# Summing z of the second attention layer over token tiles in fp32 on GpSimd and VectorE, in place of 64 one-column matmuls, with the instruction lists of all engines remade

## The chip, the cores and the metric

The kernel runs on one core of a Trainium2 chip. The metric is the device time of one execution in microseconds (us). All runs told here were in the fast state with a granted TensorE clock of 0.99 to 1.0. Of each kernel there is also one profiled execution, and the profiles and traces shown are of those. A verdict of "faster" or "slower" needs more than 2%; nothing here comes near that, so the questions are about single microseconds out of 431.

## The reference, cut to what matters

Two linear-attention blocks alternate with two feed-forward blocks, over 2048 tokens of width 512 (16 tiles of 128 tokens).

```python
phi = lambda t: jnp.where(t > 0, t + 1, jnp.exp(t)) + 1e-6
pq, pk = phi(q), phi(k)
kv = jnp.einsum("bhsd,bhse->bhde", pk, v)
z = jnp.einsum("bhsd->bhd", pk)                 # what the change is about
den = jnp.einsum("bhqd,bhd->bhq", pq, z)[..., None] + 1e-6
o = num / den
...
x = x + _A_ref(_layernorm(x, axis=-1), A_wqkv, A_wo)          # layer 0
x = x + _B_ref(_layernorm(x, axis=-1), B_w_gate, B_w_up, B_w_down)
x = x + _A_ref(_layernorm(x, axis=-1), A_wqkv, A_wo)          # layer 2
x = x + _B_ref(_layernorm(x, axis=-1), B_w_gate, B_w_up, B_w_down)
```

z is the sum of pk over all tokens: 512 numbers, one for each head and dimension.

## The kernel before

Every engine works through its own list of instructions, in order, and these lists are written out by hand in the source: one for TensorE and one each for ScalarE, VectorE, GpSimd and the DMA queue. In the names, the first figure is the layer; `2k5` is the K projection of tile 5, `2q13` a query projection, `2g5` four matmuls of pk against xn (the matrix G), `2z5` the four one-column matmuls of tile 5, `2d01` the denominators, `2m0` a part of the product M that stands behind z, `2s` the new final sum. A PSUM bank is one of the eight buffers that matmuls write.

```python
def z_acc(L, t):                    # before: 4 one-column matmuls for a tile
    if L not in zb:
        zb[L] = [bank(pin=True), 0]         # a PSUM bank held from first to last
    ...
    for c in range(NC):
        mm(pb, pk[t][:, c * P:(c + 1) * P], ones[:], n == 0 and c == 0, n == T - 1, ...)
    if n == T - 1:
        z_fin(L, pb)                        # VectorE: Zm = z masked by heads

def z_add(L, t):                    # there already, used only by the change
    eng = "dve" if f"{L}b{t}" in ON_ACT else "pool"
    if n == 1: op(eng, lambda v: v.tensor_copy(out=zs, in_=pk[t][:]), ...)
    else:      op(eng, lambda v: v.tensor_tensor(out=zs, in0=zs, in1=pk[t][:], op=ALU.add), ...)

def z_sum(L):                       # there already, used only by the change
    op("dve", lambda v: v.tensor_copy(out=hi, in_=zs), ...)                              # bf16 value
    op("dve", lambda v: v.tensor_tensor(out=lo, in0=zs, in1=hi, op=ALU.subtract), ...)   # remainder
    for i, src in enumerate((hi, lo)):
        for c in range(NC):
            mm(pb, src[:, c * P:(c + 1) * P], ones[:], i == 0 and c == 0, i == 1, ...)
    z_fin(L, pb)
```

## Time and profile before

| | before |
|---|---|
| time, first three runs | 431.31 us median (430.57 to 431.77) |
| span of the profiled run | 429.9 us |
| TensorE busy | 421.3 us, 98% |
| TensorE waits on record, all | under 6 us, in ten places |
| one-column matmuls of layer 2 | 64, worth 1.63 us of TensorE |

The spans of kernels differ by tenths, so I read them by stretches: the distance in the timeline of TensorE from the start of one named group to the start of another. A wait shows as a longer stretch; what comes before it does not matter.

The prediction shows the busy shares, the chain, the waits and the z stretch of this kernel. VectorE at the end of the first feed-forward layer's opening (columns: start, busy time, instruction, and in brackets the idle time before it with what ended it):

```profile
94.55 0.41 DVE L523 TENSOR_SCALAR xnB<-X,mv,rstd 128x512 bf16<-128x512 bf16 x1
95.92 0.43 DVE L733 TENSOR_TENSOR pq<-pq,RT 128x512 bf16<-128x512 bf16 x1 [0.96 <-DMA RT<-rrep]
...
96.97 0.69 DVE L788 TENSOR_TENSOR hT<-tht,pb 128x512 bf16<-128x512 f32 x1
```

VectorE stands 0.96 us in front of a multiplication whose operand a transposing DMA has yet to bring; hT, behind it in the list, comes late, and TensorE waits 0.81 us for it at 97.72. ScalarE behind z:

```profile
257.26 0.63 ACT L720 ACTIVATE rrep<-rtok 128x512 bf16<-128x512 bf16 x1 [0.27 <-DMA RT<-rrep]
258.52 0.63 ACT L720 ACTIVATE rrep<-rtok 128x512 bf16<-128x512 bf16 x1 [0.63 <-DMA RT<-rrep]
261.13 0.63 ACT L720 ACTIVATE rrep<-rtok 128x512 bf16<-128x512 bf16 x1 [1.99 <-DMA RT<-rrep]
261.67 1.06 ACT L658 ACTIVATE GT<-pb 128x512 bf16<-128x512 f32 x2
```

Three copies wait, 2.9 us in sum, because the DMA has not yet read the buffer that they write; the evacuations of G (line 658) stand behind them.

### The profile page before, as it was taken

What the parts mean: (1) busy time and instruction counts of PE and PEld (TensorE: products, weight loads), DVE (VectorE), ACT (ScalarE), POOL (GpSimd) and SP (SyncE); (2) the same over time, 40 slices, a digit from 0 to 9 for tenths busy, and PEclk for the clock granted to TensorE, in tenths of its full rate; (3) what the DMA queues carried; (4) which work ended last, traced back from release to release, by engine and by line L of the source; (5) the groups of instructions that cost most, each with busy time, mean ns of one, the idle gap of its engine ahead of it and who ended that gap; (6) DMA issues with size and microseconds to landing.
All of it is one profiled execution on the core that took longest, in us unless ns stands there. A gap on an engine that the chain in (4) does not pass through costs nothing.

```text
span 429.9 us, 6424 instructions
## 1 busy us (share of the span) xinstructions
PE 421.3 (98%) x2275; PEld 196.7 (46%) x2275; DVE 280.2 (65%) x625; ACT 205.1 (48%) x404; POOL 69.8 (16%) x192
## 2 busy tenths in 40 slices
PE   8999999999999999999999999999999999999997
PEld 6444444444444444444444454344444444444443
DVE  6856899884585476874545549977846606934752
ACT  5999885551375334344375747455322303411320
POOL 4534036210130130000212000431002000100000
PEclk9999999999999999999999999999999999999999
DMA  8748534522021021000011113222110010031001
GB/s 281 135 75 300 155 61 120 127 51 50 0 38 24 2 51 35 2 0 2 13 39 24 24 26 69 57 37 50 23 27 12 19 43 25 2 73 38 0 2 49
DMA packets 53279, 23.22 MB, mean 54 GB/s; under 512 B 46528, under 2 KB 52160, under 8 KB 53248
## 3 DMA queue, kind: packets, MB, share of 16 engines
q1 hardware_dynamic: 51408, 16.27, 17.9%
q0 software_dynamic: 1296, 6.03, 4.2%
q10 hardware_dynamic: 544, 0.52, 0.4%
q8 instruction: 18, 0.29, 0.3%
q14 instruction: 13, 0.11, 0.1%
HBM read 9.70 MB, written 2.10 MB: 27 GB/s over the span
## 4 chain that ended last, share of the span: by engine, by line
PE 84%; DMA 7%; DVE 4%; ACT 2%; issue 1%; POOL 1%; SPq 0%; ACTq 0%; DVEq 0%
PE pb L410 84%; DMA RT<-rrep 3%; DMA xnT<-xnB 2%; DMA xnT<-xnA 1%; DMA X<-in_A_x_dram 1%; ACT rrep L720 1%; DVE X L763 1%; DVE rtok L713 0%; DVE pq L574 0%; POOL rstd L512 0%; DVE tht L785 0%; DVE pq L751 0%; DVE xnB L523 0%; SPq L724 0%; ACT xnB L499 0%
## 5 line engine op out<-in xcount | busy, mean ns | idle before, releaser
L783 ACT ACTIVATE tht<-pb 128x512 f32<-128x512 f32 x112 | 65.0, 595 | 123.1 <-PE pb L410 90.1
L785 DVE SCALAR_TENSOR_TENSOR tht<-tht,pb 128x512 f32<-128x512 f32 x112 | 75.3, 684 | 64.7 <-ACT tht L783 60.4
L410 PE MATMUL pb<-xnT,Wg 128*128 128x512 bf16 x448 | 114.9, 379 | 1.0 <-DMA xnT<-xnB 1.0
L410 PE MATMUL pb<-xnT,Wu 128*128 128x512 bf16 x448 | 115.0, 379 | 0.0
L410 PE MATMUL pb<-Wd,hT 128*128 128x512 bf16 (+2 forms) x462 | 100.0, 373 | 0.8 <-DVE hT L788 0.8
L788 DVE TENSOR_TENSOR hT<-tht,pb 128x512 bf16<-128x512 f32 x112 | 73.8, 683 | 2.4
L410 PEld LDWEIGHTS pb<-Wd,hT 128*128 128x128 bf16 x462 | 44.5, 98 | 53.5 <-DVE hT L788 1.8
L410 PEld LDWEIGHTS pb<-xnT,Wg 128*128 128x128 bf16 x448 | 43.5, 98 | 53.9 <-DVE X L763 1.1
L410 PEld LDWEIGHTS pb<-xnT,Wu 128*128 128x128 bf16 x448 | 43.8, 98 | 52.9 <-issue 0.3
L512 POOL TENSOR_TENSOR rstd<-vpe,negh 128x1 f32<-128x1 f32 x64 | 37.2, 584 | 50.8 <-DVE vpe L508 49.2
L565 ACT ACTIVATE etmp<-pb 128x512 bf16<-128x512 f32 x64 | 37.1, 594 | 15.8 <-PE pb L410 8.8
L502 POOL TENSOR_SCALAR mv<-sums 128x1 f32<-128x1 f32 x55 | 12.9, 239 | 178.4 <-DVE X L763 91.5
L499 ACT ACTIVATE xnB<-X,sums 128x512 bf16<-128x512 bf16 x32 | 23.0, 718 | 20.4 <-DVE X L763 10.9
L410 PE MATMUL pb<-xnT,Wqkv 128*128 128x512 bf16 x128 | 32.0, 379 | 0.0
L410 PE MATMUL pb<-Wqkv,xnT 128*128 128x512 bf16 x128 | 31.2, 379 | 0.6 <-DMA xnT<-xnA 0.3
L410 PE MATMUL pb<-pk,xnA 128*128 128x512 bf16 x128 | 31.5, 378 | 0.0
L570 DVE TENSOR_SCALAR etmp<-etmp 128x512 bf16<-128x512 bf16 x64 | 18.0, 291 | 19.7 <-ACT etmp L565 19.3
L499 ACT ACTIVATE xnA<-X,sums 128x512 bf16<-128x512 bf16 x23 | 16.5, 717 | 29.2 <-DVE X L811 29.2
L410 PE MATMUL pb<-GT,pq 128*128 128x512 bf16 x128 | 30.2, 379 | 0.0
L763 DVE SCALAR_TENSOR_TENSOR X<-pb,X 128x512 bf16<-128x512 f32 x32 | 21.4, 684 | 8.2 <-PE pb L410 8.2
L811 DVE SCALAR_TENSOR_TENSOR X<-pb,X 128x512 bf16<-128x512 f32 x16 | 11.0, 689 | 19.4 <-PE pb L410 19.4
L568 ACT ACTIVATE pq<-pb,onep 128x512 bf16<-128x512 f32 x25 | 17.1, 688 | 7.3 <-PE pb L410 7.2
(70 smaller groups left out, 292.3 us busy)
## 6 DMA issues: line engine op xcount, KB each, us to landing
out_dram<-pq SPq DMA_DIRECT2D x15, 128.0 KB, 1.8
Wg<-in_B_w_gate_dram POOLq DMA_DIRECT2D x4, 448.0 KB, 5.2
Wu<-in_B_w_up_dram POOLq DMA_DIRECT2D x4, 448.0 KB, 5.2
X<-in_A_x_dram SPq DMA_DIRECT2D x6, 256.0 KB, 4.6
Wd<-in_B_w_down_dram POOLq DMA_DIRECT2D x3, 512.0 KB, 5.5
Wqkv<-in_A_wqkv_dram SPq DMA_DIRECT2D x2, 512.0 KB, 7.5
Wqkv<-in_A_wqkv_dram ACTq DMA_DIRECT2D x2, 256.0 KB, 3.5
X<-in_A_x_dram SPq DMA_DIRECT2D x4, 128.0 KB, 3.4
```

Source lines behind the costliest of these rows:

```text
L410: return op("pe", lambda e: e.matmul(o_ap, lhsT=lhsT, rhs=rhs, start=start, stop=stop, skip_group_check=skip), r=r, w=w, n=n)
L499: op("act", lambda a: a.activation(out=b_ap, in_=X[:, t, :], func=ACT.Square, scale=-float(D), bias=sums[:, t:t + 1], accum_out=mv[:, t, 1 ...
L502: op("pool", lambda p: p.tensor_scalar(out=mv[:, t, 0:1], in0=sums[:, t:t + 1], scalar1=-1.0 / D, scalar2=None, op0=ALU.mult), r=[f"sm{t}" ...
L512: op("pool", lambda p: p.tensor_tensor(out=rstd[:, t:t + 1], in0=vpe[:, t:t + 1], in1=negh[:], op=ALU.pow), r=[f"vp{t}", "negh"], w=[f"rs{ ...
L565: op("act", lambda a: a.activation(out=etmp[e][:], in_=PB[pb][:], func=ACT.Exp), r=[f"pb{pb}"], w=[f"e{e}"], kind="exp")
L568: op("act", lambda a: a.activation(out=dst, in_=PB[pb][:], func=ACT.Identity, bias=onep[:]), r=[f"pb{pb}", "onep"], w=dk, kind="id1")
L570: op("dve", lambda v: v.tensor_scalar(out=etmp[e][:], in0=etmp[e][:], scalar1=1.0, scalar2=1e-6, op0=ALU.min, op1=ALU.add), r=[f"e{e}"], w ...
L763: op("dve", lambda v: v.scalar_tensor_tensor(out=X[:, t, :], in0=PB[pb][:], scalar=1.0, in1=X[:, t, :], op0=ALU.mult, op1=ALU.add, accum_o ...
L783: op("act", lambda e: e.activation(out=tht[a][:], in_=PB[pg][:], func=ACT.Tanh, scale=0.5), r=[f"pb{pg}"], w=[f"th{a}"], kind="tanh")
L785: op("dve", lambda v: v.scalar_tensor_tensor(out=tht[a][:], in0=tht[a][:], scalar=1.0, in1=PB[pg][:], op0=ALU.add, op1=ALU.mult), r=[f"pb{ ...
L788: op("dve", lambda v: v.tensor_tensor(out=hT[h][:, j, :], in0=tht[a][:], in1=PB[pu][:], op=ALU.mult), r=[f"pb{pu}", f"th{a}"], w=[f"h{h}_{ ...
L811: op("dve", lambda v, pb=pb, lo=lo, hi=hi: v.scalar_tensor_tensor(out=o_ap[:, lo:hi], in0=PB[pb][:, 0:hi - lo], scalar=0.5, in1=X[:, t, lo ...
```

## The change

The intent: take 56 matmuls off the engine that bounds the kernel. The 16 tiles of pk are added into one fp32 tile by engines with room, the sum is split into a bf16 value and a bf16 remainder, and eight one-column matmuls do the rest. In the source only the lists change, but nearly all of them do, in all four layers. The core of the diff (cut; most changed lines are left out):

```diff
 PROGRAM (TensorE)
-1n9 1u307 ... 2k15 2k14 2g3 2g5 2q20 2z4 2q22 2k13 2q23 2z15
-2z9 2z7 2g2 2k12 2g7 2z3 2z14 2z6 2z8 2g6 2z2 2z11 2z5 2z12 2z13 2z0 2g14 2z1 2z10 2q13 2d01 2g12 2d02 ...
+1n9 1u307 ... 2k15 2k14 2g3 2g5 2q20 2q22 2k13 2q23 2g2 2k12
+2g7 2g6 2g14 2q13 2s 2d01 2g12 2d02 2g1 2d00 2d03 ...
 ORDER (VectorE, only lines with the end of the sum)
+2q22.ts 2q20.ts 2q20.phi 2k13.ts 2k13.phi 2k13.zs 2k12.ts 2q23.ts 2k12.phi 2k12.zs 2s.zh 2s.zl 2q22.phi 2z.zm
 ORDER (GpSimd, likewise)
+2x13.negm 2x13.pow 2x12.vpe 2x12.pow 2k15.zs 2k14.zs 3x0.negm 3x0.pow 3x2.negm 3x2.vpe 3x2.pow 3x1.vpe 3x1.pow
 PE_T
-0d2 0t0 0t1 0t2 0t3 2d1
+0d2 0t0 0t1 0t2 0t3 2d1 2z
 ON_ACT (additions on VectorE: 2b0 2b5 2b7 2b8 2b9 2b11 2b12 2b13; some other choices of engine change too)
```

## The prediction

> **What bounds the kernel now.** I read the page's busy shares first, then its chain of work that ended last, then the list of what TensorE waited for, then the timeline of TensorE around the place that the change touches, then the durations of single instructions.
>
> ```profile
> PE 421.3 (98%) x2275; PEld 196.7 (46%) x2275; DVE 280.2 (65%) x625; ACT 205.1 (48%) x404; POOL 69.8 (16%) x192
> ...
> PE 84%; DMA 7%; DVE 4%; ACT 2%; issue 1%; POOL 1%; SPq 0%; ACTq 0%; DVEq 0%
> ```
>
> TensorE is busy for 421.3 of 429.9 us and is 84% of the chain. The other engines have room: VectorE a third, GpSimd five sixths. So only two things count: matmul time taken away, and TensorE waits put in or taken out. These are all the waits on record before the change:
>
> ```profile
> PE pb L410 <- DVE hT L416: 1.2, 1, 1.2
> PE pb L410 <- DMA xnT<-xnB: 1.0, 2, 0.6
> PE pb L410 <- DVE pq L574: 0.8, 1, 0.8
> PE pb L410 <- DVE hT L788: 0.8, 1, 0.8
> ...
> PE pb L410 <- DVE Zm L615: 0.3, 1, 0.3
> PE pb L410 <- DVE pq L751: 0.3, 1, 0.3
> ```
>
> They sum to less than 6 us, spread over ten places. The Zm wait of 0.3 us is layer 0's, where the matmuls that read Zm stand close behind the last one-column matmul; the 1.0 us on xnT comes after the second attention layer, at 277.69 and 293.75 us. In the second attention layer's own stretch from 236 to 262 us TensorE never waits.
>
> ```profile
> 243.56 0.44 PE L410 MATMUL pb<-ones,pk 128*128 128x1 bf16 x12
> 243.87 1.02 PE L410 MATMUL pb<-pk,xnA 128*128 128x512 bf16 x4
> ...
> 246.45 0.54 PE L410 MATMUL pb<-ones,pk 128*128 128x1 bf16 x16
> 246.86 1.02 PE L410 MATMUL pb<-pk,xnA 128*128 128x512 bf16 x4
> 247.72 0.74 PE L410 MATMUL pb<-ones,pk 128*128 128x1 bf16 x24
> 248.32 1.02 PE L410 MATMUL pb<-pk,xnA 128*128 128x512 bf16 x4
> 249.18 0.34 PE L410 MATMUL pb<-ones,pk 128*128 128x1 bf16 x8
> 249.38 1.02 PE L410 MATMUL pb<-xnT,Wqkv 128*128 128x512 bf16 x4
> 250.24 0.24 PE L410 MATMUL pb<-Zm,pq 128*128 128x8 bf16 x4
> ```
>
> These are the one-column matmuls that the change removes. The second figure of a line (a busy time with a pipelined tail of some 0.14 us) overstates what a group takes. The distance from start to start is what TensorE pays: 24 of them from 247.72 to 248.32, 0.60 us or 25 ns each; four wide matmuls take 0.86 us. The last projection of four matmuls (249.38 to 250.24) stands between the end of z and the first reader of Zm, and it hides the making of Zm, which VectorE does at 249.56 in 0.21 us.
>
> **What the Trainium skill says.** "TensorE: Matmul & The Clock Gate", section "Back-to-back issue gap", gives about 60 cycles, a floor of about 25 ns, for 1 to 64 columns. The trace agrees to the nanosecond. So a one-column matmul costs its floor, and its weight load (96 ns in the rows) is hidden. "GPSIMD Engine Reference", section "3.1 Elementwise — side-by-side cycle accounting", gives about 2.6 cycles an element for an add of two tensors at 1.2 GHz; no such add is in the trace before, so I take from it an estimate of 512 x 2.6 / 1.2 = 1.1 us, some 1.2 with dispatch. "VectorE: DVE Perf Modes", section "Mode 2×_2P — use both read ports for one tensor", says that an fp32 tensor_tensor stays at one element a cycle; the trace has no fp32 add wholly in SBUF, but its one-element-a-cycle forms of 512 columns take 683 ns (hT) against 420 ns for the bf16 form (pk), so I take 0.68 us. "SBUF — State Buffer", section "SBUF: two separate sides", says that GpSimd and VectorE share a port pair under an exclusive lock, held for a whole instruction, when VectorE works in a two-port mode or with two SBUF inputs. GpSimd does only one-column work in this trace after its start, so nothing here confirms or denies what a wide add would do.
>
> ```profile
> L788 DVE TENSOR_TENSOR hT<-tht,pb 128x512 bf16<-128x512 f32 x112 | 73.8, 683 | 2.4
> ...
> L574 DVE TENSOR_TENSOR pk<-pk,etmp 128x512 bf16<-128x512 bf16 x21 | 8.7, 420 | 0.1
> ...
> L615 DVE TENSOR_TENSOR Zm<-pb,mask 128x32 bf16<-128x32 f32 x2 | 0.4, 206 | 2.9 <-PE pb L410 2.9
> ```
>
> **The change part by part.**
>
> Removed: 64 one-column matmuls (16 tiles by four chunks) of layer 2. Added: eight (four chunks for the value, four for the remainder). Adding the start-to-start distances of all six runs in the full timeline (4, 12, 16, 24 and 8 matmuls: 0.11 + 0.31 + 0.41 + 0.60 + 0.20) gives 1.63 us for 64; eight cost 0.20. TensorE gains 1.43 us.
>
> Added beside it: sixteen running additions into one fp32 tile, in one serial chain across two engines. Despite the change's name, the list of engines in the diff sends tiles 0, 5, 7, 8, 9, 11, 12 and 13 to VectorE; only eight, among them the first copy, go to GpSimd. GpSimd gets about 8 x 1.1 = 9 us, spread over 80 us in which it is nearly idle. VectorE gets 8 x 0.68 = 5.4 us, plus the rounding to bf16 (about 0.42, estimated from the two-port 405 ns copies) and the subtraction (0.68): 6.5 us, also where it has room (7.5 us of 14.2 busy from 236 to 250 us). None of this lies on TensorE until the end of the chain.
>
> The end of the chain does. The last tile is 12, whose projection TensorE ran at 244.73. In the new order it comes about 0.42 us earlier, because the 16 one-column matmuls in front of it are gone: 244.31, with its end in PSUM near 245.35. Then ScalarE needs 0.6 for exp and about 0.6 for the shifted copy (queued), VectorE 0.42 for the maximum (ends near 247.0), 0.68 for the last addition (247.7), 0.42 for the rounding (248.1) and 0.68 for the remainder (248.8). TensorE, with 56 matmuls fewer, gets to the eight at about 248.6. Their second half waits for the remainder, some 0.2 us. Then the change loses its cover: the last query projection is now placed ahead of the eight and the first reader of Zm right behind them. So a bare round is added: matmul drain 0.16, Zm 0.21 and hand-overs of 0.05, after a 0.42 us maximum that stands on VectorE ahead of Zm. Zm is ready near 249.4, and its reader starts near 249.45, against 250.24 before. An unhindered reader would have started at 248.8. So about 0.65 us of the 1.43 goes into a new wait, and about 0.8 us is left.
>
> Moved: nearly every list of order was made anew, also in layers where no operation changes. The start has the same 61 filler matmuls, six of them moved ahead of the first transpose; ScalarE takes three instead of two G evacuations of layer 2 and takes them ahead of part of the reciprocal's copies, which in the trace before made the chain wait at 261 us; some normalizations change engine. Each can move one of the ten waits by tenths either way. I give them 0 on average and a spread of about 0.8 us.
>
> Sum: 431.3 - 1.43 + 0.65 = 430.5 us.
>
> **The rivals.** (A) The additions come late. The chain alternates: after tile 11 on VectorE, GpSimd adds 15 and 14, then VectorE 13 and 12. By my count tile 11 is in at about 242.1, GpSimd's two end near 244.5, and VectorE needs that by about 246. There is about 1.4 us of slack; with additions of 2 us instead of 1.2, or held up by the port lock, it is gone, each further 0.5 us becomes TensorE wait, and the time is 431 to 432.5. Against it: GpSimd's rows show it idle there. (B) The gain is taken back behind. From 250 to 294 us the chain before runs through VectorE, ScalarE and transposing DMAs, with 1.3 us of TensorE waits in it; if those depend on things that did not come earlier, the 0.8 us shows up again as longer waits, and the time stays at 431.3. Against it: the same chain starts from this layer's den matmuls, which do come 0.8 us earlier. (C) The new order heals waits beyond z, such as part of the 0.8 us on pq in layer 0 or the 0.6 us on xnT: 429.5. (D) The port lock delays VectorE's two-input work in the feed-forward stretch from 160 to 208 us, where the first additions fall and VectorE is 70% busy, until PSUM buffers run out and TensorE stalls: 433 or more. Against it: VectorE's own work there reads PSUM on one side, so it has one SBUF input.
>
> **Range and chances.** The terms that I can size give 430.5. A and B pull up by 0.5 to 1.5, C down by about 1; D is unlikely. The three runs before spread over 1.2 us already. I take 429.2 to 432.1 for eight in ten. Two per cent are 8.6 us, six times the whole gain, and only a stall that no row hints at could cost as much: faster 0.01, same 0.97, slower 0.02.
>
> **What would show it right or wrong.** Right: eight one-column matmuls in layer 2, 0.2 us in all; a new TensorE wait on Zm (and perhaps on the remainder tile in GT) of 0.4 to 1.0 us in sum near 249 us; its reader 0.6 to 1.0 us earlier against its surroundings than before; GpSimd rows of eight wide operations of 1.0 to 1.4 us; VectorE busy time up by about 6 us with no effect on the span; TensorE busy time down by about 1.4. Wrong: a wait of over 1.5 us there with GpSimd adding until 246 us or later would be rival A; an unchanged span with longer waits after 260 us, rival B; a fall of over 2 us, or new waits in layers 0, 1 and 3, would mean that the reordering and not z decides.

## More of the kernel before

The head is all that runs before layer 2's first K projection.

Behind z, the reciprocals of the denominators are widened by ScalarE and turned by transposing DMAs, through three buffers:

```python
rrep = [sb("rrep", [P, 512], BF16) for _ in range(3)]
...
for tl in range(TG):
    q = r_rrep.take()                                   # ring of 3
    op("act", ... activation(out=rrep[q] ..., in_=rtok[d] ..., func=ACT.Copy), kind="rep")
    op("sp", ... dma_start(RT[R][:, :, ...], rrep[q][:], transpose=True), dma=True, kind="rT")
```

## The result, and the profile after

| | before | after |
|---|---|---|
| time, runs of the same rounds | 430.94 us median of 4 (430.0 to 431.77) | 428.98 us median of 4 (428.8 to 429.14) |
| ratio of fast runs | | 0.9955, 95% interval 0.9932 to 0.9978 |
| TensorE busy | 421.3 us | 420.3 us |
| VectorE / GpSimd busy | 280.2 / 69.8 us | 289.8 / 79.7 us |
| span of the profiled run | 429.9 us | 427.0 us |

A ratio is the mean time of one kernel's fast runs over the mean of the other's fast runs of the same rounds, so it is not quite the ratio of the medians quoted. The result lies within 2%, as predicted, and 0.2 us under the low end of the range. Two repeats of the changed kernel (below) gave 429.36 and 429.82 us, which are inside it. The centre of 430.5 was too high by 0.7 to 1.5 us in all three.

The page's shares and chain, and the waits of TensorE (columns: waiter, releaser, us in total, times, longest):

```profile
PE 420.3 (98%) x2219; PEld 196.1 (46%) x2219; DVE 289.8 (68%) x632; ACT 203.3 (48%) x401; POOL 79.7 (19%) x202
...
PE 87%; DMA 6%; DVE 3%; ACT 2%; issue 1%; POOL 1%; SPq 0%; POOLq 0%; DVEq 0%; ACTq 0%
```

```profile
PE pb L410 <- DVE hT L416: 1.2, 1, 1.2
PE pb L410 <- DVE Zm L615: 0.6, 2, 0.4
PE pb L410 <- DMA xnT<-xnA: 0.5, 1, 0.5
PE pb L410 <- DVE pq L751: 0.3, 1, 0.3
PE pb L410 <- DVE pq L574: 0.2, 1, 0.2
PE pb L410 <- ACT xnT L551: 0.2, 1, 0.2
PE pb L410 <- DVE GT L634: 0.2, 1, 0.2
```

TensorE has 56 matmuls less and is a larger share of the chain, so waits have gone. Compared with the list in the prediction, the 1.0 us on xnT<-xnB and the 0.8 us on hT L788 are gone, and the 0.8 us on pq L574 has shrunk to 0.2. None of these three stands in the z stage, and one pair of traces doesn't tell a lasting change from scatter: in the second trace of the changed kernel (run 5) the wait on pq L574 is 0.7 us again. The z stage itself, in the timeline of TensorE:

```profile
246.57 1.03 PE L410 MATMUL pb<-xnT,Wqkv 128*128 128x512 bf16 x4
247.43 0.24 PE L410 MATMUL pb<-ones,GT 128*128 128x1 bf16 x4
247.84 0.25 PE L410 MATMUL pb<-ones,GT 128*128 128x1 bf16 x4 [0.17 <-DVE GT L634]
248.48 0.24 PE L410 MATMUL pb<-Zm,pq 128*128 128x8 bf16 x4 [0.39 <-DVE Zm L615]
```

From the first of the eight matmuls to the first reader of Zm it takes 1.05 us (247.43 to 248.48), where the matmuls alone need 8 x 25 ns = 0.20. So 0.85 us is lost here, in a wait for the remainder and a bare round through VectorE. The new instructions by the tile that they write (columns: instruction, count, duration in ns as min/median/max, first and last start):

```profile
L627 DVE TENSOR_TENSOR GT<-GT,pk x8: 683/688/693, 148.9 to 245.9; 128x512 f32<-128x512 f32 x8
L627 POOL TENSOR_TENSOR GT<-GT,pk x7: 1153/1156/1283, 169.7 to 241.9; 128x512 f32<-128x512 f32 x7
L633 DVE CAST GT<-GT x1: 426/426/426, 246.6 to 246.6; 128x512 bf16<-128x512 f32 x1
L634 DVE TENSOR_TENSOR GT<-GT x1: 693/693/693, 247.1 to 247.1; 128x512 bf16<-128x512 f32 x1
```

Where did the time come from? The starts of the last wide matmul group differ by 2.89 us in the two traces, and they split like this:

| stretch of TensorE, start to start | before | after | difference |
|---|---|---|---|
| begin to first K projection of layer 2 | 121.69 | 120.20 | -1.49 |
| to K projection of tile 4 of layer 2 | 79.90 | 79.86 | -0.04 |
| to first reader of Zm (the z stage) | 48.65 | 48.42 | -0.23 |
| to first down projection of layer 3 | 59.91 | 58.72 | -1.19 |
| to the last group of at least twenty down matmuls | 104.46 | 104.52 | +0.06 |

The stage that the change is named after gave 0.23 us. The rest lies in the first two layers, where no operation changed, and behind z. One pair of traces is not enough for this: the first stretch alone took between 120.52 and 123.12 us in the nine traces taken with the old lists there. So the experiments ask which part of the new lists carries the gain.

### The profile page after: what moved, and what is told of

Read it like the earlier page. It is cut to its first block, busy times and chain, and to the rows that moved or that the text cites. A ratio compares the mean times of both kernels' runs of the same rounds, so it can differ in the third digit from the quotient of the medians.

```text
span 427.0 us, 6344 instructions
## 1 busy us (share of the span) xinstructions
PE 420.3 (98%) x2219; PEld 196.1 (46%) x2219; DVE 289.8 (68%) x632; ACT 203.3 (48%) x401; POOL 79.7 (19%) x202
## 3 DMA queue, kind: packets, MB, share of 16 engines
q1 hardware_dynamic: 51408, 16.27, 17.4%
## 4 chain that ended last, share of the span: by engine, by line
PE 87%; DMA 6%; DVE 3%; ACT 2%; issue 1%; POOL 1%; SPq 0%; POOLq 0%; DVEq 0%; ACTq 0%
PE pb L410 87%; DMA xnT<-xnA 2%; DMA Wo<-in_A_wo_dram 1%; DMA Wu<-in_B_w_up_dram 1%; DMA X<-in_A_x_dram 1%; DMA RT<-rrep 1%; DVE X L763 0%; ACT etmp L565 0%; DVE pq L574 0%; POOL rstd L512 0%; DVE pq L751 0%; ACT rrep L720 0%; DVE rtok L713 0%; ACT xnB L499 0%; ACT xnA L499 0%
## 5 line engine op out<-in xcount | busy, mean ns | idle before, releaser
L788 DVE TENSOR_TENSOR hT<-tht,pb 128x512 bf16<-128x512 f32 x112 | 74.4, 682 | 3.2
L508 POOL TENSOR_SCALAR vpe<-mv 128x1 f32<-128x1 f32 x34 | 7.6, 223 | 88.8 <-ACT xnB L499 78.9
```

The lines of the kernel that those rows point to most:

```text
L508: op(vp_on, lambda p: p.tensor_scalar(out=vpe[:, t:t + 1], in0=var, scalar1=scale, scalar2=1e-5, op0=ALU.mult, op1=ALU.add), r=[vk], w=[f" ...
L788: op("dve", lambda v: v.tensor_tensor(out=hT[h][:, j, :], in0=tht[a][:], in1=PB[pu][:], op=ALU.mult), r=[f"pb{pu}", f"th{a}"], w=[f"h{h}_{ ...
```

## The experiments

The theory at this point: z itself gives a few tenths, and the remade order elsewhere gives the rest. The rival: z's 64 matmuls do cost what they seem to, and the order is noise. All kernels gave correct results except where said; each was timed in five rounds. "Before" of a job is the mean of the 11 runs of the kernel before on the same chip, and it lay between 431.07 and 431.75 us.

**1. The new order without z.** The changed kernel's lists, with the additions taken out and the 64 matmuls put back in their old places between the projections.

```diff
-2k13 2q23 2g2 2k12 2g7 2g6 2g14 2q13 2s 2d01
+2k13 2q23 2z15 2z9 2z7 2g2 2k12 2g7 2z3 2z14 ... 2z1 2z10 2q13 2d01      # and no .zs, no 2z in PE_T
```

> Every new list of order and engine of the changed kernel, but z of layer 2 by its 64 one-column matmuls, at the places that they had before. Theory O (the new order brings most of the 1.96 us, and z by itself almost nothing, because in the trace of the changed kernel the stretch from the last query projection of group 1 to the first reader of Zm is only 0.23 us shorter than before): 1.5 to 2.0 us below the kernel before, so 429.0 to 429.5, and within 0.5 of the changed kernel. Theory Z (the 56 matmuls saved carry the gain, and what the trace shows ahead of layer 2 is the scatter of the kernel before): 0.6 us or less below the kernel before.

Measured: 434.23 us (432.58 to 438.2), ratio 1.0073 [1.0038, 1.0108]. Slower, a miss. TensorE stands 1.59 us in front of a query projection that the changed kernel runs without a wait:

```profile
244.24 1.02 PE L410 MATMUL pb<-xnT,Wqkv 128*128 128x512 bf16 x4 [1.59 <-DVE pq L577]
```

A projection needs a PSUM bank; z by matmul pins one of eight from its first tile to its last while G pins four, so the bank's previous reader (pq, line 577) decides. The z stage took 50.68 us against 48.65, and there was a further loss behind z (60.44 us against 58.72).

**2. The old order with z added.** The kernel before, with the additions put at places of my choosing and the eight matmuls in place of the 64.

```diff
+2x14.pow 2k10.zs 2x15.negm 2x15.pow 2k6.zs 2x13.vpe ...    # GpSimd: one of my insertions
```

> The kernel before with its own order, and only z of layer 2 taken over: the sixteen additions on the same engines as in the changed kernel, set in behind each tile's phi, the eight one-column matmuls right behind the last query projection, as in the changed kernel. Theory O: 0 to 0.5 us below the kernel before (a gain of 1.43 us in matmuls, a new wait of about 0.9 to 1.2 us at Zm). Theory Z: 1.0 to 1.8 us below.

Measured: 436.83 us (434.98 to 438.43), ratio 1.0123 [1.0098, 1.0148]. A miss through my own placing. GpSimd works in order, and I had put the addition of tile 6, whose operand came late, in front of the normalization of tile 13. ScalarE then stood 4.61 us and TensorE 2.36:

```profile
236.96 1.15 POOL L628 TENSOR_TENSOR GT<-GT,pk 128x512 f32<-128x512 f32 x1 [5.61 <-DVE pk L575]
238.20 0.19 POOL L509 TENSOR_SCALAR vpe<-mv 128x1 f32<-128x1 f32 x1
...
239.32 0.26 POOL L517 TENSOR_SCALAR nmr<-mv,rstd 128x1 f32<-128x1 f32 x1
```

```profile
239.62 0.81 ACT L520 ACTIVATE xnA<-X,nmr,rstd 128x512 bf16<-128x512 bf16 x1 [4.61 <-POOL nmr L517]
```

It shows that an engine at 16% of its time is not free: a late operand blocks all that stands behind it. The placing on GpSimd alone is not the fault, though: the changed kernel has this addition at the same place of GpSimd's list (`2x15.pow 2k6.zs 2x13.vpe`). There the new list of VectorE takes `2k6.phi`, which makes the operand, ahead of `2x15.apply`, `1n13.res` and `1n12.res`, and normalizes tile 13 itself, where ScalarE did it here. So the run doesn't measure z alone; it is a first sign that z needs the remade lists around it.

**3. One move of the early order.** The kernel before, with the multiplication that held VectorE at 95.92 put four instructions later, much as the changed kernel has it.

```diff
-0d3.pqn2 1u009.gst 1u009.h 1u110.gst 1u110.h 0d3.pqn ...
+1u009.gst 1u009.h 1u110.gst 1u110.h 0d3.pqn2 0d3.pqn ...
```

> The kernel before with one single instruction moved on VectorE: a multiplication of group 3 of layer 0 by its reciprocal (it waits for a transposing DMA) goes behind the next two feed-forward tiles instead of ahead of them, as in the changed kernel. In the trace before, VectorE stands there until 95.9 us, and TensorE waits 0.81 us for hT at 97.7 us; in the changed kernel this wait is gone. Theory O: that wait of 0.8 us goes and the time falls by 0.6 to 1.0 us. Theory Z: no change beyond 0.3 us.

Measured: 431.71 us (430.41 to 432.23), ratio 1.0001 [0.9982, 1.002]. The wait on hT is gone from the trace, and the stretch around it is 3.40 us instead of 4.01, but the time shows nothing. Inconclusive: 0.6 us is about what the interval can hide, and other traces of the old list have that stretch at 3.02 to 4.25 without any move. The wait comes in some executions of that list and not in others: in three of the eight traces with this part of the old list unmoved (0.81, 0.83 and 0.98 us), and in none of the nine with the new list.

**4. 56 of the 64 matmuls left out, nothing else.** The kernel before with z summed over two tiles only. The result is wrong (relative error 1.26).

```diff
-2z4 ... 2z15 2z9 2z7 ... 2z3 2z14 2z6 2z8 ... 2z2 2z11 2z5 2z12 2z13 2z0 ... 2z1 2z10
+2z1 2z10
```

> The kernel before with 14 of the 16 tiles left out of z of layer 2, so that 56 one-column matmuls go and nothing is added; the result is wrong on purpose. It measures the gross value of the removal. If what TensorE saves there reaches the end: 1.2 to 1.6 us below the kernel before (56 times 25 ns is 1.43). If the chain behind it (VectorE, ScalarE and the transposing DMAs from 250 to 294 us) takes it back (rival B of the prediction): 0 to 0.6 us below, with longer waits for xnT at the start of the second feed-forward layer.

Measured: 429.06 us (428.63 to 429.97), ratio 0.9941 [0.9923, 0.996]. The z stage is 47.26 us, 1.39 less than before; 56 x 25 ns is 1.40 (the 1.43 in the expectation is a slip). So the matmuls cost exactly their floor, and the rest of the 2.5 us in the time, which is more than either expectation had, lies elsewhere (the stretch behind z was 58.98 against 59.91; in another trace with all the matmuls and the old lists there, run 7's, it was 59.27). Had the changed kernel kept all of this, it would have gained 1.4 us in the stage; it kept 0.23.

**5. The changed kernel again**, to know its own scatter.

> The changed kernel as it is, once more, as the base of this group and as a second trace of the same program. It tells how much of the gain ahead of layer 2 is scatter between executions: in the traces so far the point where the first feed-forward layer starts lies between 68.1 and 69.2 us for kernels with the same code up to there. All theories: 1.5 to 2.5 us below the kernel before (428.8 to 429.7). If the head of the run is scatter, the start of layer 2's first projection moves by 0.5 us or more against the first trace of the changed kernel, while the stretch of layer 2 and its aftermath repeat within 0.2 us.

Measured: 429.36 us (429.05 to 429.62), ratio 0.9946 [0.9919, 0.9972]. The second half of its trace agrees with the first one's to 0.01 us (291.52 us from the first K projection of layer 2 to the last group of down matmuls in both).

**6. The new order with the 64 matmuls in one block.** As run 1, but all of them directly ahead of the last query projection, so that their bank is pinned for a short time.

```diff
-2g7 2g6 2g14 2q13 2s 2d01
+2g7 2g6 2g14 2z2 2z0 2z1 2z3 2z4 2z8 2z7 2z10 2z5 2z6 2z9 2z11 2z15 2z14 2z13 2z12 2q13 2d01
```

> The new lists of order with z of layer 2 by 64 one-column matmuls, as in the first try of this, but all of them in one block right ahead of the last query projection, so that the PSUM bank of z is held for 3 us and not for 9. In the first try a query projection waited 1.6 us for a PSUM bank. Theory O (order brings most): 1.0 to 2.0 us below the kernel before, at most 0.7 us above the changed kernel. Theory P (z of the change is worth its 1.4 us of matmuls plus a PSUM bank set free, and the order alone is worth nothing): 0.5 us or less below the kernel before. The stretch from the projections of tile 15 to the first reader of Zm says it apart from the end time: 11.4 to 11.7 us if the bank was the only trouble of the first try, over 12.5 if not.

Measured: 431.85 us (430.45 to 432.27), ratio 1.0000 [0.9973, 1.0026]. The z stage is 48.67 us, as before, so the 2 us of run 1 were the pinned bank, as far as moving the matmuls shows it. But the stretch behind z took 60.38 us against 58.72: the remade order behind z is bad for a kernel with the matmuls. The new order is not good in itself; it is fitted to the new z.

**7 and 8. The new order of the first two layers alone, and everything else alone.** Run 7 has the new lists up to the seam in layer 1 and the old ones, with the 64 matmuls, after it. Run 8 has the old head and the new z and the new rest.

```diff
# run 7: lists of the change up to 2d0/1x10-1u102 in layers 0 and 1, lists of before behind
# run 8: the reverse
```

> The kernel before with the new order of layers 0 and 1 only (up to the point where the first tiles of the first feed-forward layer are written back); layer 2 with its z and layer 3 in their old order. Theory O: 0.7 to 1.3 us below the kernel before, by the wait for hT at 97 us that goes. Theory P: within 0.5 us of the kernel before.

> The reverse: the old order of layers 0 and 1, then z as changed and the new order of the rest. Theory O: 0.7 to 1.3 us below the kernel before. Theory P: 1.7 to 2.3 us below, the whole gain.

Measured: 429.70 us (429.15 to 431.1), ratio 0.9958 [0.9932, 0.9984], and 429.55 us (428.99 to 430.73), ratio 0.9953 [0.9927, 0.9978]. Each half alone gives about 2 us by the clock, the whole gives 2.3 in the same job; the halves do not add. With intervals of 1.1 us each, the clock cannot split the gain. What it does show is that the head, in which nothing about z changed, is worth something: run 7's interval excludes 1. But run 8, with the old head, shows by the clock the whole gain (theory P's figure), and run 7 more than theory O gave it; neither theory had both.

**9 and 10. The z stage alone, and the order behind it alone.** Run 9 has the new lists from layer 1's seam to the first reader of Zm, run 10 only those behind it.

```diff
# run 9:  head before | z stage after  | rest before
# run 10: head before | z stage before | rest after
```

> Only the middle part is new: from the write-back of the first feed-forward tiles to the making of Zm (the z sum as changed, with the new order around it); head and aftermath of Zm (group reciprocals, GT, output projection, layer 3) in the old order. In the traces so far the stretch from the projections of tile 15 on to the first reader of Zm is 11.96 us old and 11.56 new, the one from that reader to the first write-back of layer 3 is 59.3 to 59.9 us old and 58.7 new. Theory O (z by itself is worth 0.2 us, the rest is order): 0 to 0.5 us below the kernel before; aftermath 59.3 us or more. Theory P (with z shorter, the waits behind it shrink too, as where 56 matmuls were dropped: aftermath 59.0): aftermath 59.0 or less and 0.8 us or more below the kernel before.

> Only the last part is new: the order behind Zm of layer 2; z by its 64 matmuls and the head as before. Theory O: the aftermath takes 58.7 to 58.9 us and the time is 0.6 to 1.2 us below the kernel before. Theory P: aftermath 59.3 or more, within 0.4 us of the kernel before. A third outcome is an aftermath of over 60 us, as in the two tries of the new order with z by matmuls (60.4): then the new order behind Zm rests on the PSUM bank that the z sum sets free, and neither can be had without the other.

Measured: 432.56 us (430.72 to 433.5), ratio 1.0033 [1.001, 1.0057], and 433.02 us (430.6 to 435.1), ratio 1.0046 [1.0016, 1.0076]. Either part alone is a loss by the clock. In run 9 the z stage is 48.44 us, the same 0.2 better as in the changed kernel. Behind it TensorE waits 1.76 us for a transposed xnT, but that stretch is only 0.38 us longer than before (60.29 against 59.91); most of what this trace loses (1.56 us) lies in its head, which took 123.12 us against 121.69 and was 1.27 us late already at the first gate matmul of layer 1, under unchanged lists. So where run 9's loss comes from is not shown. In run 10 the head was faster than before (120.73 us) and the loss lies behind z, where the stretch took 62.06 us against 59.91: ScalarE stands there, then TensorE:

```profile
259.53 1.57 ACT L658 ACTIVATE GT<-pb 128x512 bf16<-128x512 f32 x3
262.45 0.63 ACT L720 ACTIVATE rrep<-rtok 128x512 bf16<-128x512 bf16 x1 [1.34 <-DMA RT<-rrep]
...
265.07 1.57 ACT L658 ACTIVATE GT<-pb 128x512 bf16<-128x512 f32 x3
```

```profile
263.12 1.04 PE L410 MATMUL pb<-Wo,KVT 128*128 128x512 bf16 x4
...
265.72 4.78 PE L410 MATMUL pb<-GT,pq 128*128 128x512 bf16 x12 [0.93 <-ACT GT L658]
...
279.39 1.02 PE L410 MATMUL pb<-xnT,Wg 128*128 128x512 bf16 x4 [0.31 <-DMA xnT<-xnB]
```

The same list in the changed kernel reaches that copy without a wait, and evacuates M 0.46 us after its matmuls began instead of 1.95:

```profile
258.74 1.57 ACT L658 ACTIVATE GT<-pb 128x512 bf16<-128x512 f32 x3
260.18 0.64 ACT L720 ACTIVATE rrep<-rtok 128x512 bf16<-128x512 bf16 x1
...
262.79 1.60 ACT L658 ACTIVATE GT<-pb 128x512 bf16<-128x512 f32 x3
```

**11. The cover given back.** (Cover: matmuls that keep TensorE busy while another engine makes what it needs next.) The changed kernel with four G matmuls between the last projection and the eight (so that the remainder is ready), and four behind them (so that Zm is).

```diff
-2g7 2g6 2g14 2q13 2s 2d01 2g12 2d02 2g1 2d00 2d03
+2g7 2g6 2g14 2q13 2g12 2s 2g1 2d01 2d02 2d00 2d03
```

> The changed kernel with one group of four wide matmuls (of G) moved ahead of the eight one-column matmuls and one moved between them and the first reader of Zm, so that the remainder and Zm are made under TensorE's work again, as they were before. The step of the prediction on lost cover says that the two waits there (0.17 on the remainder, 0.39 on Zm, and the gaps round them, 0.85 us in all from the eight to the reader) are due to the place and not to the additions being late: they go, and the time is 0.4 to 0.8 us below the changed kernel (428.6 to 429.0). If the additions are late (rival A of the prediction), the wait stays and moves to the eight: within 0.2 us of the changed kernel.

Measured: 428.92 us (428.49 to 429.42), ratio 0.9951 [0.9932, 0.997]. In the timeline the eight run in one piece and nothing waits:

```profile
247.90 1.03 PE L410 MATMUL pb<-pk,xnA 128*128 128x512 bf16 x4
248.76 0.34 PE L410 MATMUL pb<-ones,GT 128*128 128x1 bf16 x8
248.97 1.02 PE L410 MATMUL pb<-pk,xnA 128*128 128x512 bf16 x4
249.82 0.98 PE L410 MATMUL pb<-Zm,pq 128*128 128x8 bf16 x28
```

**12. All sixteen additions on VectorE.**

```diff
-2k2.phi 1n7.res ... 2k0.phi 2k0.zs ...      # and 8 .zs in GpSimd's list
+2k2.phi 1n7.res ... 2k0.phi 2k2.zs 2k0.zs ...
```

> The changed kernel with all sixteen additions on VectorE, none on GpSimd. In the trace of the changed kernel VectorE's bf16 normalization of a tile takes 1.26 us instead of 0.41 where it falls on a GpSimd addition, and TensorE stands 0.16 us at 243.0 us behind such a lengthened stretch. Theory L (the lock on the port pair that the Trainium skill describes costs in this chain): no operation of 1.26 us is left, the gap at 243 us goes, and the time is 0.1 to 0.4 us below the changed kernel although VectorE has 5 us more to do. Rival: VectorE becomes late with the end of the chain (8 more additions of 0.61 us), the wait before Zm grows by 0.3 us or more, and the time is above the changed kernel.

Measured: 430.49 us (429.83 to 431.86), ratio 0.9993 [0.997, 1.0016], against 428.92 of the kernel of run 11 in the same job and 429.0 to 429.8 of the changed kernel. VectorE falls behind in the stretch where K and the feed-forward block overlap (first K tile 4 to G of tile 3: 37.24 us against 36.86). GpSimd's half of the work is worth having, though each of its additions takes 1.7 times as long. TensorE waits for VectorE at two places where the changed kernel's trace has no wait:

```profile
182.58 1.02 PE L410 MATMUL pb<-xnT,Wqkv 128*128 128x512 bf16 x4 [0.31 <-DVE tht L785]
227.16 2.75 PE L410 MATMUL pb<-Wqkv,xnT 128*128 128x512 bf16 x12 [0.39 <-DVE pk L577]
...
236.65 1.89 PE L410 MATMUL pb<-Wqkv,xnT 128*128 128x512 bf16 x8
```

Theory L was half right. No normalization (line 523) took more than 0.43 us here, where two of the changed kernel took 1.26; and from the query projection ahead of the K matmuls of the third line (235.79) to the first reader of Zm it took 14.01 us against 14.32, because two gaps of TensorE are gone (below). But the two waits shown cost more than that.

**13 to 16. The buffers behind z, and the cover beside the changed kernel.** What was still open: why the order behind z is so sensitive, and whether the cover's gain is real. Runs 13 and 14 lend a fourth buffer to the copies of the reciprocal (an idle feed-forward tile, for there was no memory left for one more), in run 10's kernel and in the kernel before.

```diff
-q = r_rrep.take()
+q = r_rrep.take() if L == 0 or g == 3 else r_rrep4.take()      # Ring(4)
+rb = rrep[q] if q < 3 else tht[NTH - 1][:].bitcast(BF16)
```

> The kernel before with only the order behind the first reader of Zm remade, and now a fourth buffer for the copies of the reciprocal (rrep) of layer 2's first two DMA groups, lent by an idle tile of the feed-forward block. With three buffers this mixture was 2 us slower than before: ScalarE stood 1.34 us in front of such a copy because an earlier copy's transposing DMA had not yet read its buffer, the evacuation of M behind it came late, and M to the first gate matmul of layer 3 took 16.27 us. Theory T (too few rrep buffers in an in-order ScalarE make the loss): that wait is gone, M to gate falls to 13 to 14 us, and the time falls by 1.5 us or more, to a ratio of 0.995 to 1.001 to before. Theory U (the transposes themselves land late and the wait only moves to their reader on VectorE): the stretch stays above 15.5 us and the ratio at 1.003 to 1.006.

> The kernel before with the same fourth rrep buffer and nothing else. In its trace ScalarE waits 2.9 us in three pieces for these DMAs between 257 and 261 us, and the stretch from the first reader of Zm to the first gate matmul of layer 3 takes 27.45 us against 26.78 in the changed kernel. Theory T: this is where the 0.7 to 1 us behind z comes from, so the fourth buffer alone takes the stretch to 26.7 to 26.9 and the time 0.5 to 0.9 us below before. Theory U: the wait goes to another engine, the stretch stays at 27.2 to 27.6 and the time within 0.3 us of before.

Measured: in run 10's kernel 430.87 us (430.01 to 432.4), ratio 1.0002 [0.9976, 1.0027], down from 1.0046. From M to the first gate matmul it takes 13.23 us instead of 16.27, and ScalarE evacuates M 0.46 us after its matmuls began. Theory T holds for that kernel: three buffers in front of an in-order ScalarE made the loss.

```profile
264.24 0.66 ACT L723 ACTIVATE rrep<-rtok 128x512 bf16<-128x512 bf16 x1
264.76 1.60 ACT L659 ACTIVATE GT<-pb 128x512 bf16<-128x512 f32 x3
```

In the kernel before, the same edit gave 433.12 us (430.91 to 434.45), ratio 1.0039 [1.0011, 1.0067]: slower, which neither theory had. The wait did not go; it moved, and the evacuations of G still stand behind it:

```profile
260.67 0.63 ACT L723 ACTIVATE rrep<-rtok 128x512 bf16<-128x512 bf16 x1 [2.99 <-DMA RT<-rrep]
261.20 1.07 ACT L659 ACTIVATE GT<-pb 128x512 bf16<-128x512 f32 x2
```

With four buffers, this copy (the second of its group in ScalarE's list) writes the buffer whose DMA is the last of the first group's four in the queue; with three it was that of the third. The stretch from Zm to the first gate matmul became 28.12 us instead of 27.45. So the number of buffers is not what separates before from after; the order of copies against the order of DMAs is part of it.

The last pair is the kernel of run 11 and the changed kernel.

> The changed kernel with four G matmuls between the last projection and the eight z matmuls, run again beside the changed kernel itself. If the cover's 0.7 us, seen in one trace from the z stage to the end, is real, its mean lies 0.4 to 0.9 us below that of the changed kernel of this same job. If something behind it gives it back, the two agree within 0.2 us.

> The changed kernel once more: 428.8 to 429.6 us, a ratio of 0.994 to 0.997 to before, as in its first two jobs. It is here to be compared with the run with the cover.

Measured: with the cover 429.35 us (427.85 to 430.4), ratio 0.9956 [0.9934, 0.9978]; the changed kernel 429.82 us (428.88 to 430.22), ratio 0.9968 [0.995, 0.9987]. The means differ by 0.53 us, 429.22 against 429.75, with scatter as large as that; the clock alone would not settle it. The traces do, for the second half: from the first K projection of layer 2 to the last group of down matmuls it is 290.81 us in both traces with the cover, and 291.52, 291.52 and 291.62 in the three traces of the changed kernel. The cover is worth 0.7 to 0.8 us there, and nothing behind gives it back. It is the fastest version tried, by that reading.

## Why the prediction was right or wrong

**Right: the matmuls and their price.** 25 ns each (run 4: 1.39 us for 56), eight in 0.20 us. (The prediction speaks of six groups of them; it adds five, and the sum is right.)

**Right: the additions and their chain.** GpSimd 1.156 us where 1.1 to 1.2 was estimated, VectorE 0.688 for 0.68, rounding 0.426 for 0.42 (the 405 ns behind that estimate are those of normalizations, line 523, not of copies), remainder 0.693 for 0.68. The last addition ran from 245.90, and the remainder began at 247.09, on time for the wait of 0.17 us on it that was predicted as 0.2. Rival A did not occur. VectorE's busy time rose by 9.6 us, not by 6 to 6.5: the new instructions are 6.6 of it, and two lengthened normalizations (below) 1.7. No run isolates what this cost.

**Mis-sized: what z leaves.** The prediction kept 0.8 us of 1.43; the stage kept 0.23. The loss at Zm was 0.85 us, not 0.65. Two gaps on TensorE that the prediction did not have, of 0.17 us at 235.9 and 0.16 us at 243.0, take 0.33 more; 1.43 - 0.85 - 0.33 = 0.25. The first is a weight load that waits for a transposed xnA; the second, as I read its releasers, lies behind a PSUM bank that VectorE freed late, with slow operations of its own beside GpSimd's last two additions. Both are gone in run 12, where GpSimd adds nothing (14.01 us for 14.32), so they come with GpSimd's share of the additions. The port lock, which the prediction called unlikely to matter (rival D), fits: two normalizations, which take 0.41 us in the trace before, took 1.26 when they began beside a GpSimd addition, and none did in run 12. The prediction's argument against D looked only at instructions that read PSUM; these read SBUF alone. First VectorE, then GpSimd, of the changed kernel:

```profile
227.79 1.26 DVE L523 TENSOR_SCALAR xnA<-X,mv,rstd 128x512 bf16<-128x512 bf16 x1
...
230.95 1.26 DVE L523 TENSOR_SCALAR xnA<-X,mv,rstd 128x512 bf16<-128x512 bf16 x1
```

```profile
227.75 1.15 POOL L627 TENSOR_TENSOR GT<-GT,pk 128x512 f32<-128x512 f32 x1 [0.64 <-DVE GT L627]
...
230.90 1.15 POOL L627 TENSOR_TENSOR GT<-GT,pk 128x512 f32<-128x512 f32 x1
```

It cost 0.3 us in this stage, not the 2 us of rival D. This error alone would have made the prediction too low, not too high.

**The step that failed: "I give them 0 on average".** The remade lists were taken as noise around zero, to be added to z's own gain. In the changed kernel they were worth about 1.5 us, and rival C, which the prediction put at 429.5, is what happened (of its two examples the waits on xnT went for good, the one on pq came back in run 5). In numbers over all traces: up to the first K projection of layer 2, nine traces with the old head average 121.56 us (standard deviation 0.81; one of them has the single move of run 3) and nine with the new head 120.86 (0.53), a gain of 0.7 with a standard error of 0.3. Behind z, up to the first down projection of layer 3, the four traces with old z and old order took 59.91, 59.27, 59.94 and 58.98 us (before, runs 7, 3 and 4, the last with most of z left out), on average 59.53; the new ones took 58.72, 58.77, 58.72 and 58.80 (after, runs 8, 5 and 16), on average 58.75, a gain of 0.8 (1.0 without run 4). This part belongs to lists and z together: with the old z the new lists took 60.38 to 62.06 us there (runs 1, 6 and 10), with the new z in other surroundings the old lists took 59.45 and 60.29 (runs 2 and 9). With z's 0.23 this makes 1.7 us; the three ratios of the changed kernel (0.9955, 0.9946, 0.9968) average to 0.9956, or 1.9 us. The two waits on xnT<-xnB that the prediction listed (1.0 us) are the part behind z that can be pointed at: traces with old z and old lists there have 0.5 to 1.0 us of this wait (before, runs 3, 4 and 7), and the three of the changed kernel and that of run 8 have none.

Rival B, that the gain is taken back behind, did not occur in the changed kernel, but runs 9 and 10 show how near it was: z without its new surroundings, or the surroundings without z, both lose by the clock. The lists were made for each other, so "order" and "z" cannot be given shares that hold in any other kernel.

**Left open.** Why the first two layers are faster by 0.7 us is not settled: the one move tried (run 3) took its wait away and did not show in the time. That wait, in three of the nine traces with the old head, makes up some 0.3 us of the 0.7 (an estimate: 2.6 us in all, over nine). Run 8 shows the whole gain by the clock without the new head, so that the head's share rests on run 7's interval and on a difference of means of some two standard errors. Behind z, run 13 shows the mechanism in the mixed kernel, not in the kernel before, where run 14 went the other way. That a pinned bank made the loss in run 1 rests on run 6, which moved the matmuls as well as shortened the pinning.

## What to carry to other kernels

Where each engine works through a fixed list, a change that comes with remade lists has two effects, and the list can be the larger one: separate them by running the new lists with the old operation and the reverse, and don't take a mixture's time for a share: some mixtures here were worse than both kernels (runs 1, 9 and 10), others gained nearly all (runs 7 and 8). Work taken off the bounding engine is only worth what is left of the cover at the place where its result is read; here moving two groups of four wide matmuls (run 11) returned 0.7 to 0.8 us, more than the change's own stage had kept. A side engine with much idle time still works in order: look at what stands behind the instruction that is put there, and at what it locks.

## What the Trainium skill lacked or had wrong

- "SBUF — State Buffer", section "SBUF: two separate sides": it says that GpSimd and VectorE share a port pair under an exclusive lock, held for a whole instruction, and that the other fully blocks. The lock fits what is seen here: two VectorE normalizations of 128x512 bf16 that began 0.04 and 0.05 us after a GpSimd addition of 1.15 us took 1.26 us instead of 0.41, and none did once GpSimd added nothing (run 12). But they ended 0.15 us after the addition; had all of their 0.41 us waited for its end, they would have taken 1.52 (an estimate from these numbers). The page has no duration for such a pair.
- "GPSIMD Engine Reference", section "3.1 Elementwise — side-by-side cycle accounting": its 2.6 cycles an element gave an estimate of 1.1 us for 512 columns; measured 1.153 to 1.283, median 1.156. Nothing wrong; the page names a dispatch term for GpSimd without a figure, which by this difference is some 0.05 us (an estimate).
- "DMA: Bandwidth & Descriptors" gives a rate for transposing DMAs but not the time of one small one from SBUF to SBUF. Here, of 128x512 bf16, the issues of one queue took 1.19 us or more each, and one landed 2.4 us after its issue in the middle and 4.1 us at worst (changed kernel, behind z). That is how long a buffer that a copying engine wrote stays taken.
